# Decode attention with a 805 MB cache on one core: longer runs per transfer, all queries at the start, and another exit

## The chip, the cores and the metric

One Trainium2 chip, one of its cores. The metric is device time in microseconds (us) of one execution. A time is the median of a kernel's runs. Each ratio is the mean time of one kernel's fast runs over the mean of the other's fast runs of the same rounds, so it isn't quite the ratio of the medians quoted beside it. The profile measures a span that is 1.8 us shorter than the time of the same run.

## The reference

One token goes through a pre-norm attention block with a cache of 32,768 keys and values for each of 32 heads, then through a small MLP. All inputs are bf16.

```python
B, Sq, D = 1, 1, 640
H, Sk, Dh = 32, 32768, 192
q = (layernorm(x) @ wq).reshape(B, Sq, H, Dh).transpose(0, 2, 1, 3)
scores = einsum("bhqd,bhkd->bhqk", q, k_cache) * (Dh ** -0.5)
o = einsum("bhqk,bhkd->bhqd", softmax(scores), v_cache)
h = x + o.transpose(0, 2, 1, 3).reshape(B, Sq, H * Dh) @ wo
out = h + relu(layernorm(h) @ w1) @ w2          # w1 640 x 1536
```

K and V of all heads are 2 x 32 x 32,768 x 192 x 2 B = 805 MB. With the weights, 825 MB are read once, and nothing large is written.

## The kernel before

Each engine runs its own program. SyncE issues all loads in one order and waits where a place isn't free. GpSimd passes landings on to TensorE and VectorE. A load holds 64 keys a partition, 24 KB in one run (JL = 64). There are four key places and two value places, and a head takes four loads of each kind. A head's scores are made in eight chunks of 32 keys a partition: 16 or 20 of them on TensorE, from transposed keys that ScalarE copies out of PSUM, and the rest on VectorE. ScalarE makes the exponentials, TensorE the products with the values.

```python
kt = [sbuf(f"kt{i}", [P, JL * Dh], bf16, 512) for i in range(NL)]     # NL = 4
vt = [sbuf(f"vt{i}", [P, JL * Dh], bf16, 512) for i in range(NV)]     # NV = 2
wq_s = sbuf("wq_s", [P, DT * QG * Dh], bf16, 512)                     # wq for 8 heads
...
load(wq_v, wq_view[:, :, 0:QG * Dh], "dwq", "wq", 0)
for h in range(H):
    for ld in range(NL if h < LAST else NL - 1):
        n = NL * h + ld
        load(kt[ld][:], rows(k_hd, h, P * JL * ld, JL), f"dk{ld}", "k", h, ld)
        if n >= NV:
            hp, lp = divmod(n - NV, NL)
            g.wait("PV", hp, 2 * lp + 1)           # products out of this place are done
        load(vt[ld % NV][:], rows(v_hd, h, P * JL * ld, JL), f"dv{ld % NV}", "v", h, ld)
        # ... wq for the next 8 heads, wo for two heads
# ... the last head: the last quarter in pieces of 40, 16, 8 keys, then their values, then w1, w2
g.wait("y_row")
load(out.rearrange("b s (c p) -> (b s c) p", p=P), y_row[:], "dout", "out")
g.wait("out")
```

TensorE's order in a head puts the value products of a chunk right behind the next chunk's transposes:

```python
for c in range(NC):
    transposes(g, h, c)
    if c > 0:
        values(g, h, c - 1)
    else: ...                                       # last chunk of the head before, denominators
    scores_pe(g, h, c)
    # c == 5: q of the next head, c == 6: its broadcast
```

At the end, a context manager (`nc.cleanup_on_exit()`) clears the semaphores after a barrier behind everything else.

The softmax here doesn't subtract the row's maximum and nothing guards it: scores larger than these inputs give would overflow.

## Time and profile before

| | before |
|---|---|
| time, first three runs | 1923.66 to 1923.92 us |
| span of the profile | 1922.4 us |
| bytes read | 825 MB |
| packets on the load queue | 44,762 |
| first data packet to last w2 packet | 1912.87 us |
| last w2 packet to the output's issue | 4.12 us |
| output's issue to end of span | 3.35 us |

Rows five and six are read from the trace's DMA records: each packet has a start, a duration and a size. They split a span into loading, what comes after it, and what the engines lose between. On the page itself, a row of 9s for the DMA with lower shares for all engines says who is the bound. A queue that waits long for compute says nothing against that as long as transfers are still in flight.

### The profile page before, as it was taken

How to read it: one execution, taken by the hardware profiler on the slowest of the kernel's cores; microseconds unless marked ns; L12 is line 12 of the kernel's file. 1: busy time of each engine (PE TensorE's matmuls, PEld its weight loads, DVE VectorE, ACT ScalarE, POOL GpSimd, SP SyncE). 2: the span in 40 equal slices, each digit the busy share in tenths (PEclk: the TensorE clock that was granted, in tenths of full speed). 3: DMA queues.
4: the chain of work that ended last, by engine and by line, in shares of the span. 5: the costliest groups of instructions: out<-in, count | busy, mean ns of one | idle time of the engine just before them, and what ended most of it. 6: DMA issues, size and time to landing. Idle time of an engine off the chain costs nothing.

```text
span 1922.4 us, 36522 instructions
## 1 busy us (share of the span) xinstructions
PE 1563.5 (81%) x15899; PEld 1073.1 (56%) x15899; DVE 1560.6 (81%) x734; ACT 970.7 (50%) x2031; POOL 0.7 (0%) x6
## 2 busy tenths in 40 slices
PE   5888888788888888788787888888878887888887
PEld 4555555555555555555555555555545555555555
DVE  5878888887887888787888878888778887888886
ACT  3555455454555555454454555545445454555554
POOL 0000000000000000000000000000000000000000
PEclk9898888988888898888898888888888888898888
DMA  9999999999999999999999999999999999999998
GB/s 405 430 431 432 432 434 433 433 431 432 433 431 433 434 433 432 432 432 428 435 434 433 432 432 433 433 432 432 432 433 433 432 433 433 432 433 433 433 430 342
DMA packets 44793, 825.26 MB, mean 429 GB/s; under 512 B 4580, under 2 KB 6116, under 8 KB 12132
## 3 DMA queue, kind: packets, MB, share of 16 engines
q1 hardware_dynamic: 44762, 824.99, 99.9%
q8 instruction: 12, 0.20, 0.0%
q14 instruction: 9, 0.07, 0.0%
q10 hardware_dynamic: 10, 0.00, 0.0%
HBM read 824.97 MB, written 0.00 MB: 429 GB/s over the span
## 4 chain that ended last, share of the span: by engine, by line
DMA 76%; PE 21%; SPq 2%; issue 1%; ACT 0%; POOLq 0%; DVE 0%
DMA kt<-in_A_k_cache_dram 76%; PE o_ps L324 11%; PE tp L343 10%; SPq L224 2%; PE sp L324 0%; PE attT L324 0%; ACT kT L538 0%; POOLq L306 0%; PE mm L324 0%; DVE o_pair L638 0%; ACT pB L544 0%; PE mm L527 0%; DVE y_row L713 0%; ACT h1T L600 0%; DVE oT L648 0%
## 5 line engine op out<-in xcount | busy, mean ns | idle before, releaser
L623 DVE TENSOR_TENSOR pr<-kt,qb 128x2304 f32<-128x2304 bf16 (+2 forms) x257 | 756.0, 2942 | 278.9 <-POOLq L290 261.5
L538 ACT COPY kT<-tp 128x1024 bf16<-128x1024 bf16 (+1 forms) x899 | 818.8, 992 | 319.3 <-PE tp L343 317.3
L343 PE MATMUL tp<-ident_f,kt 128*128 128x128 f32 x3459 | 569.7, 331 | 334.3 <-POOLq L306 334.3
L626 DVE TENSOR_REDUCE sc<-pr 128x12 f32<-128x2304 f32 (+2 forms) x257 | 755.3, 2939 | 8.9
L343 PEld LDWEIGHTS tp<-ident_f,kt 128*128 128x128 f32 x3459 | 496.1, 172 | 351.3 <-POOLq L306 350.1
L324 PE MATMUL o_ps<-vt,pB 128*2 128x384 bf16 x2286 | 472.5, 358 | 6.8 <-POOLq L306 6.6
L324 PE MATMUL o_ps<-vt,pA 128*2 128x384 bf16 x1778 | 331.0, 326 | 0.0
L324 PEld LDWEIGHTS o_ps<-vt,pB 128*2 128x2 bf16 x2286 | 184.5, 89 | 244.7 <-issue 88.3
L544 ACT ACTIVATE pB<-sp 128x20 bf16<-128x20 f32 (+2 forms) x258 | 47.9, 186 | 504.5 <-PE sp L324 504.5
L324 PEld LDWEIGHTS sp<-qm,kT 128*128 128x128 bf16 x6918 | 193.3, 97 | 77.9 <-issue 65.2
L324 PEld LDWEIGHTS o_ps<-vt,pA 128*2 128x2 bf16 x1778 | 150.7, 85 | 144.9 <-issue 7.9
L324 PE MATMUL sp<-qm,kT 128*128 128x2 bf16 x6918 | 212.0, 164 | 3.1 <-ACT kT L538 2.4
L553 ACT ACTIVATE pA<-sc 128x12 bf16<-128x12 f32 (+2 forms) x257 | 53.4, 208 | 106.4 <-DVEq L65 104.7
L544 ACT ACTIVATION_READ_ACCUMULATOR pB<-sp 128x1 f32 x258 | 50.2, 195 | 0.0
L553 ACT ACTIVATION_READ_ACCUMULATOR pA<-sc 128x1 f32 x257 | 48.7, 190 | 0.0
L631 DVE TENSOR_REDUCE rec<-mm 128x1 f32<-128x20 f32 x32 | 5.7, 179 | 50.3 <-PE mm L324 49.8
L324 PE MATMUL mm<-wq_s,xn_ln 128*1 (+1 forms) x160 | 18.7, 248 | 4.0 <-POOLq L306 4.0
L638 DVE TENSOR_SCALAR o_pair<-o_ps,rec 2x384 bf16<-2x384 f32 x32 | 19.4, 605 | 2.7 <-PE o_ps L324 1.7
L324 PE MATMUL attT<-oT,wo_s 128*128 128x1 bf16 x465 | 15.9, 163 | 0.3 <-DVE oT L648 0.3
L324 PEld LDWEIGHTS mm<-dsums,ones_mat 128*128 128x128 f32 x64 | 9.5, 188 | 10.7 <-issue 9.3
L324 PEld LDWEIGHTS attT<-oT,wo_s 128*128 128x128 bf16 x465 | 13.8, 96 | 0.4 <-DVE oT L648 0.4
L324 PE MATMUL mm<-ones_row,row_e 1*128 1x1 bf16 x384 | 14.0, 159 | 0.0
(71 smaller groups left out, 144.9 us busy)
## 6 DMA issues: line engine op xcount, KB each, us to landing
kt<-in_A_k_cache_dram SPq DMA_DIRECT2D x127, 3072.0 KB, 22.5
vt<-in_A_v_cache_dram SPq DMA_DIRECT2D x127, 3072.0 KB, 15.6
wq_s<-in_A_wq_dram SPq DMA_DIRECT2D x4, 1920.0 KB, 21.0
wo_s<-in_A_wo_dram SPq DMA_DIRECT2D x16, 480.0 KB, 16.3
kt<-in_A_k_cache_dram SPq DMA_DIRECT2D x1, 1920.0 KB, 20.2
kt<-in_A_v_cache_dram SPq DMA_DIRECT2D x2, 960.0 KB, 24.8
kt<-in_B_w_dram SPq DMA_DIRECT2D x1, 1920.0 KB, 18.5
wq_s<-in_B_w_dram SPq DMA_DIRECT2D x1, 960.0 KB, 20.5
```

Of the source, the lines that this page charges most:

```text
L224: g.do(lambda: nc.sync.dma_start(out=dst, in_=src), sem, label, by=16)
L324: return lambda: pe.matmul(o, lhsT=w, rhs=r, **kw)
L343: calls.append(lambda b=b, o=o: pe.transpose(out=dst[:, b, :], in_=src[:, o:o + 2 * P].bitcast(f32), identity=ident_f[:]))
L538: g.do(lambda: act.copy(out=kT[c % 2][:, b0:b0 + nb, :], in_=src[:, 0:nb, :].bitcast(bf16)), "act_pe", ("cp", h, c, k))
L544: g.do(lambda: act.activation(out=pB[c % 4][:, 0:jp], in_=sp[:, 0:jp], func=F.Exp, scale=SCALE, accum_out=dsums[:, 2 * c + 1:2 * c + 2]), ...
L553: g.do(lambda: act.activation(out=pA[c % 4][:, 0:jd], in_=sc[c % NC][:, 0:jd], func=F.Exp, scale=SCALE, accum_out=dsums[:, 2 * c:2 * c + 1 ...
L623: g.chain(lambda: dve.tensor_tensor(out=pr[:, 0:j1 - j0, :], in0=src[:, (off + j0) * Dh:(off + j1) * Dh].rearrange("p (j d) -> p j d", d=D ...
L626: g.chain(lambda: dve.reduce_sum(out=sc[c % NC][:, j0:j1], in_=pr[:, 0:j1 - j0, :], axis=X), "dve")
L631: g.chain(lambda: dve.reduce_sum(out=rec[:, 0:1], in_=mm[:, 0:2 * NCM], axis=X), "dve")
L638: g.do(lambda: dve.tensor_scalar_mul(out=o_pair[:, :, 1, :], in0=o_ps[0:2, 0:2 * Dh].rearrange("q (i d) -> q i d", i=2), scalar1=rec[0:2, ...
```

## The change

Its intent: fewer and longer runs in each transfer, wq out of the loop so that its place can go to keys and values, and a shorter end. The key places become two of 48 KB (128 keys a partition), the values get one place of 48 KB (`va`, the second half of a head) and one of 24 KB (`vb`, used twice a head). All of wq is loaded first, into places that keys and values will take over, and all 32 queries are made at once. In the last head all keys are loaded ahead of three quarters of the values. ScalarE copies the output and sends it, and the semaphores are cleared while it flies.

```diff
-    kt = [sbuf(f"kt{i}", [P, JL * Dh], bf16, 512) for i in range(NL)]
-    vt = [sbuf(f"vt{i}", [P, JL * Dh], bf16, 512) for i in range(NV)]
-    wq_s = sbuf("wq_s", [P, DT * QG * Dh], bf16, 512)
+    kt = [sbuf(f"kt{i}", [P, JK * Dh], bf16, 512) for i in range(NK)]      # JK = 128, NK = 2
+    va = sbuf("va", [P, JK * Dh], bf16, 512)
+    vb = sbuf("vb", [P, JL * Dh], bf16, 512)
...
+    wq_c = [kt[1][:, c * H * Dh:(c + 1) * H * Dh] for c in range(DT - 1)] + [va[:, 0:H * Dh]]
...
+        def keys(h, ld):
+            if h > 0:
+                if ld == 0:
+                    g.wait("PV", h - 1, 4 if h == 1 else 2)
+                else:
+                    g.wait("PV", h - 1, 5)
+                g.wait("scs", h - 1, 4 * ld + 3)
+            elif ld == 1:
+                g.wait("att0")
+            load(kt[ld][:], rows(k_hd, h, P * JK * ld, JK), f"dk{ld}", "k", h, ld)
+
+        def vals(h, ld):
+            if ld == 1:
+                g.wait("PV", h, 1)
+            elif h > 0:
+                g.wait("PV", h - 1, 3 if ld == 0 else NC - 1)
+            src = rows(v_hd, h, P * JK * (ld // 2), JK)
+            if ld < 2:
+                src = src[:, ld * JL * Dh:(ld + 1) * JL * Dh]
+            load((vb, vb, va)[ld][:], src, "dva" if ld == 2 else "dvb", "v", h, ld)
+
+        for c in range(DT):
+            load(wq_c[c], wq_view[:, c * H * Dh:(c + 1) * H * Dh], f"dwq{c}", "wq", c)
+        for h in range(LAST):
+            keys(h, 0)
+            vals(h, 0)
+            keys(h, 1)
+            for ld in ((2, 1) if h == 0 else (1, 2)):
+                vals(h, ld)
...
+    SUMS = ((), (), (0,), (1,), (), (), (2, 3), (4,), (5, 6, 7))            # products by slot
...
+        g.wait("yT")
+        g.do(lambda: act.copy(out=y_row[:], in_=mm[0:DT, 0:P]), "act_row", ("y_row",))
+        g.wait("y_row")
+        g.do(lambda: act.dma_start(out=out.rearrange(...), in_=y_row[:]), "dout", ("out",), by=16)
...
-    ctx.enter_context(nc.cleanup_on_exit())
+    nc.clear_and_free_semaphores([n for n in nc.allocated_since(before) if n != sems["dout"].num])
+    nc.sync.wait_ge(sems["dout"], 16)
+    nc.sync.sem_inc(sems["dout"], -16)
```

Cut from the diff: the rewritten spreading of a query, TensorE's and ScalarE's orders in the last head, VectorE's signal `scs` that it has read a key place, and GpSimd's identity of another width.

## The prediction

> **What bounds the kernel now.** I read the page's utilisation rows and DMA part first, then the chain, then the issuing queue's own waits, then timelines of the two ends.
>
> ```profile
> span 1922.4 us, 36522 instructions
> PE 1563.5 (81%) x15899; PEld 1073.1 (56%) x15899; DVE 1560.6 (81%) x734; ACT 970.7 (50%) x2031; POOL 0.7 (0%) x6
> DMA  9999999999999999999999999999999999999998
> GB/s 405 430 431 432 432 434 433 433 431 432 433 431 433 434 433 432 432 432 428 435 434 433 432 432 433 433 432 432 432 433 433 432 433 433 432 433 433 433 430 342
> DMA packets 44793, 825.26 MB, mean 429 GB/s; under 512 B 4580, under 2 KB 6116, under 8 KB 12132
> q1 hardware_dynamic: 44762, 824.99, 99.9%
> DMA 76%; PE 21%; SPq 2%; issue 1%; ACT 0%; POOLq 0%; DVE 0%
> ```
>
> No compute engine is full, and the sixteen DMA engines are: every slice but the first and last moves 428 to 435 GB/s. The chain names key transfers and then two PE groups, the transposes and the value products. That PE part is not the bound: the next view shows the queue waiting for buffers, with transfers still in flight.
>
> ```profile
> SPq L224 <- PE o_ps L324: 1772.9, 126, 33.6
> ...
> kt<-in_A_k_cache_dram SPq DMA_DIRECT2D x127, 3072.0 KB, 22.5
> vt<-in_A_v_cache_dram SPq DMA_DIRECT2D x127, 3072.0 KB, 15.6
> ```
>
> A 3072 KB load takes 3.146 MB / 433 GB/s = 7.3 us alone, so 22.5 and 15.6 us from issue to landing are about three and two loads deep. The long wait of the issuing queue is back-pressure. The two ends are where the DMA does not run:
>
> ```profile
> 0.00:3.00 3.00, 0.00 (x0) 0.00 (x0) 1.32 (x8) 1.28 (x1) 0.70 (x6) 1.00 0.28 44
> ...
> 1912.00:1916.00 4.00, 3.10 (x85) 2.75 (x85) 1.56 (x11) 0.29 (x1) 0.00 (x0) 1.00 0.46 168
> 1916.00:1920.00 4.00, 2.12 (x61) 1.75 (x61) 0.44 (x2) 0.27 (x1) 0.00 (x0) 0.57 0.00 0
> 1920.00:1924.00 4.00, 0.00 (x0) 0.00 (x0) 0.00 (x0) 0.00 (x0) 0.00 (x0) 0.50 0.00 0
> ```
>
> (The last three fields are granted clock, DMA share, GB/s.) A share of 0.28 of 3 us puts the first byte at 3 - 0.84 = 2.16 us. The packet records of the trace, laid on that, end with w2 at 1915.03 us on the slowest engine (1912 + 0.46 x 4 = 1913.8 on the mean). Between, the same records leave 1.0 us of idle DMA in all. So the span is 2.2 us of start, 1912.9 of DMA, and 7.4 of end. Only three things can shorten it: less DMA time for the same bytes, less end, less start.
>
> **What a packet costs.** In the trace's packet records, the time from one packet's start to the next on the same engine is 908.4 ns for 24,576 B, 569.5 for 15,360, 146 for 3,840, 118 for 3,072, about 50 for 1,280, and 5.85 for the 4 B semaphore write. From 118 to 908.4 the slope is 790.4 ns / 21,504 B = 0.03676 ns a byte, or 27.2 GB/s an engine; what is left over is 908.4 - 24,576 x 0.03676 = about 4.9 ns a packet, whatever its size. The 24,576 B period is 908 to 909 ns from the 5th to the 95th percentile: HBM never holds it up.
>
> **What the Trainium skill says.** "DMA: Bandwidth & Descriptors", section Where 436 GB/s comes from: 16 ports x 32 B x 850 MHz = 435.2 GB/s. The trace agrees: 16 x 27.2 = 435.2, and whole slices lie just below. The same page, Why small descriptors are slow, gives a fixed overhead of some 3 cycles a packet; the trace has 4.9 ns, about 4 cycles of that clock. The section Why a DMA increments its semaphore by 16 says that one descriptor moves one contiguous run, and trouble with runs begins beyond 64 KiB; 49,152 B is below, but no packet of the kernel before is over 24,576 B on this queue, so its trace doesn't show it. Issuing engines are not separate DMA queues: a transfer issued by ScalarE runs on the same engines, so the output gains no bandwidth from that. The output is 1.2 KB; that is no matter here.
>
> **The change part by part.** Bytes stay the same (the same caches, weights and output).
>
> Packets. Before: 31 heads x 8 loads x 128 = 31,744 of 24 KB, 1,664 in the last head, wq 2,560, wo 2,048, w1 640, w2 1,536: 40,192 and some 4,565 semaphore writes, which is the page's 44,762. After: a head has K, K and the second value half as 3 x 128 packets of 48 KB and two value quarters as 2 x 128 of 24 KB: 640 instead of 1,024, over 31 heads 19,840. The last head has 1,792 (one value quarter split in two), wq 640 of 12,288 B, the rest as it was: 26,496 in all. 13,696 fewer x 4.9 ns / 16 engines = 4.2 us. Loads fall from 285 to 194: 91 x 16 semaphore writes x 5.85 ns / 16 = 0.5 us. As the DMA sets the pace, both come off in full: **-4.7 us**.
>
> The queries. Before, each head had 5 products with wq (0.57 us in the timeline), a ScalarE row copy of 0.3 and 13 small products (0.7). After, 320 products at the start and 8 small ones a head. The 60 w1 products took 1.67 us, 28 ns each, so 64 for the last wq piece are 1.8 us after its landing, and the other 256 lie under the wq loads. All of wq now stands ahead of the keys: 7.86 MB / 434 GB/s = 18.1 us, so the first keys land at some 35 us instead of 16. The PE starts later; the DMA doesn't: **0**. The relief of about 1 us a head on PE is off the path: **0**.
>
> The end. Before, all through the last 35 us PE works without a break in the chain (keys at 1883.66, last product at 1911.6), and then come the reduction, projection and MLP:
>
> ```profile
> 1911.62 0.60 DVE L638 TENSOR_SCALAR o_pair<-o_ps,rec 2x384 bf16<-2x384 f32 x1 [1.67 <-PE o_ps L324]
> ...
> 1914.34 1.65 PE L324 MATMUL o_ps<-xn_ln,kt 128*128 128x1 bf16 x60
> ...
> 1916.36 1.75 PE L324 MATMUL attT<-h1T,wq_s 128*128 128x1 bf16 x60 [0.36 <-ACT h1T L600]
> ...
> 1918.77 0.28 DVE L713 CAST y_row<-mm 5x128 bf16<-5x128 f32 x1 [0.47 <-PE mm L527]
> 1919.08 0.36 SPq L224 DMA_DIRECT2D out_dram<-y_row  x1
> ```
>
> The output is issued 4.05 us after the DMA's last byte: the tail is PE's. After, all keys of the last head are loaded before three quarters of its values, so what follows the last value bytes is only two small products. Call the DMA's end D. The last values land 3.93 MB (w1, w2) = 9.1 us before D. VectorE is the doubt: at 0.42 us a key (5.1 us for 12), its 76 to 80 keys of the last three quarters, behind a start at the first keys' landing 60 us before D, end some 10 us before D. Then 16 + 8 keys of products (1.4 + 0.8 us), so the last product is at about D - 6; 2.7 us on is w1's turn (1911.6 to 1914.34 above), D - 3.3; 2.0 us for it and the ReLU, D - 1.3; the w2 products 1.75, held at the end by w2's last landing, D + 0.7; 1.0 for y, its transpose and the copy: D + 1.7 to 2.3 with some throttling, for 4.05 now. **-2.1 us**.
>
> After the issue. Before: issue at 1919.08, end of span 1922.4, 3.3 us: 0.4 of issue, 0.8 of wait for the landing, then 0.7, 0.6 and 0.5 of barrier waits in the queue's own view, one after the other. After, barriers and clearing run while the output flies, and its semaphore alone is waited for. The longer of the two, some 2.1, remains, and ScalarE's issue is a shade slower (0.58 us for x at the start): **-0.8 us**. Copy by ScalarE (0.2 to 0.3) for VectorE (0.28): 0.
>
> **Does the queue run dry?** This is the decision. Larger places mean fewer ahead. Set one head's first key landing at 0: K takes 14.5 us, a quarter 7.2, so V0 lands at 7.2, K1 at 21.7, V1 at 28.9, V2 at 43.4, the next keys at 58. The tight wait is V1, which needs products 0 and 1 out of the same buffer. VectorE: chunk 0 to 5.2, 0.9 for the denominators, chunk 1 (6.7) to 12.8; its exponential to 13.2; products 1 to about 16. Issue and first byte take 1.2 us (0.97 to 2.16 at the start), so data can flow at 17.2, before 21.7: **4.5 us in hand**. The next K0 needs products 2, near 37, before 42: 5. K1 needs products 5, near 52, before 64: 12. But PE has four value groups after V2's landing at 43.4, with a mean of 3.16 us each (803 us / 254) plus two score groups of 0.85: to 58, just when the next keys land. So PE can be a few us late in throttled stretches, and the 4.5 us swallow it. I set **+0.5 us** for some heads that miss.
>
> **Sum.** -4.7 - 2.1 - 0.8 + 0.5 = -7.1 on 1923.79: 1916.7; I say 1916.5.
>
> **Rivals.** One: the 48 KB run is cut in two or more packets. Against it is only the 64 KiB statement. Then the 11,904 packets of the full heads come back, 3.6 us: about 1920. Two: the V1 wait bites. For it: PE's tight stretch, clock dips to 0.54 in 3 us windows. Each us missed a head is 31 us of time: at 1 us a head 1948, at 1.3 slower by 2%. Against: the 4.5 us. Three: VectorE is late in the last head, where keys come back to back, and the tail stays as it is: 1918.6. Four: a 48 KB pitch disturbs HBM; the flat 908 ns speak against it.
>
> **Range and chances.** At best, tail and barriers give 2 more: 1913.5. With rival one, or small misses, 1920 to 1922. Range 1913 to 1922. A gain of 2% is 38.5 us, more than all DMA idle and overhead together (9.6 us at the ends, 14 of packets and semaphore writes): 0.01. Slower by 2% needs 1.3 us of dry queue in each head: 0.04. Within: 0.95.
>
> **What would show it.** Packets on the queue near 26,500 + 3,100 = 29,600 (about 41,500 if cut); steady slices of 433 to 434 GB/s; DMA's end near 1910; output issued 1.7 to 2.3 us after it; span end 2.5 after issue; the first keys transposed near 35 us. Wrong if slices fall to 425 or less in mid-run, with the issuing queue's wait on the value products ending just as the engines stop.

## The result

| | before | after |
|---|---|---|
| time, six runs each | 1923.86 us (1923.65 to 1924.11) | 1918.95 us (1917.64 to 1921.12) |
| ratio | | 0.9975, 95% interval 0.9963 to 0.9988 |
| span of the profile | 1922.4 | 1916.6 |
| load packets | 44,762 | 29,600 |
| first data packet to last w2 packet | 1912.87 | 1909.47 |
| last w2 packet to the output's issue | 4.12 | 2.80 |
| output's issue to end of span | 3.35 | 2.31 |

The gain is a quarter of a per cent here, and it is outside the noise. With 15 further runs of the same kernel beside the experiments, on three chips, the median of all 21 is 1918.33 us (1916.72 to 1921.12). The kernel before had 1923.53 to 1924.89 in all its runs. What the kernel after brings besides the gain is a spread of 4.4 us.

The page of the kernel after, the same parts as those that the prediction shows:

```profile
span 1916.6 us, 36108 instructions
PE 1560.1 (81%) x15899; PEld 1093.9 (57%) x15899; DVE 1561.3 (81%) x731; ACT 938.7 (49%) x2000; POOL 1.0 (0%) x6
GB/s 409 427 435 429 429 437 429 437 434 432 436 432 435 432 433 430 434 432 437 435 430 436 433 432 434 435 429 435 431 437 435 431 435 433 432 436 432 429 432 362
DMA packets 29634, 825.29 MB, mean 431 GB/s; under 512 B 3115, under 2 KB 4652, under 8 KB 8108
q1 hardware_dynamic: 29600, 824.98, 99.8%
DVE 39%; DMA 38%; PE 16%; ACT 5%; issue 1%; DVEq 0%; POOLq 0%; SPq 0%
```

Busy times are nearly unchanged (ScalarE's falls from 970.7 to 938.7). There are a third fewer packets for the same bytes, and the mean rate rises from 429 to 431 GB/s. The chain now names VectorE first, at 39%. That doesn't make VectorE the bound: the load queue now also waits for VectorE's signal that a key place is read, so the chain goes back through it. The queue's own waits show the same thing, and its transfers are as deep in flight as before (a 6144 KB load alone takes 14.5 us):

```profile
SPq L232 <- PE o_ps L360: 1198.2, 126, 24.2
SPq L43 <- DVEq L65: 462.1, 49, 11.8
...
kt<-in_A_k_cache_dram SPq DMA_DIRECT2D x62, 6144.0 KB, 26.7
```

The end, in order of time (start, duration, engine, line, operation):

```profile
1906.85 0.60 DVE L715 TENSOR_SCALAR o_pair<-o_ps,rec 2x384 bf16<-2x384 f32 x1 [1.66 <-PE o_ps L360]
...
1911.59 1.72 PE L360 MATMUL attT<-h1T,kt 128*128 128x1 bf16 x60 [0.36 <-ACT h1T L673]
...
1913.98 0.26 ACT L676 CAST y_row<-mm 5x128 bf16<-5x128 f32 x1 [2.44 <-PE mm L592]
1914.26 0.29 ACTq L678 DMA_DIRECT2D out_dram<-y_row  x1
```

From the last product (o_pair) to the output's issue it is 7.4 us here and 7.5 before, the same work. What moved is where it stands against the last loads.

A middle head, to hold against the prediction's picture of one head. The first line is the landing of its first keys as TensorE sees it, the second the issue of its second value load, the third the landing of its second keys:

```profile
919.75 6.02 PE L379 MATMUL tp<-ident_f,kt 128*128 128x128 f32 x27 [2.71 <-POOLq L342]
...
936.02 0.33 SPq L232 DMA_DIRECT2D vb<-in_A_v_cache_dram  x1
...
941.55 3.46 PE L379 MATMUL tp<-ident_f,kt 128*128 128x128 f32 x15 [3.60 <-POOLq L342]
```

Issued 16.3 us after the first keys (predicted 17.2 less 1.2 of issue, so 16), with the other keys landing at 21.8 (predicted 21.7). The 2.71 in the bracket is TensorE's idle time ahead of the keys: it wasn't late there.

### The profile page after: what moved, and what is told of

Same layout as the page of the kernel before. It is cut to its first block, busy times and chain, and to the rows that moved or that the text cites. A ratio compares the mean times of both kernels' runs of the same rounds, so it can differ in the third digit from the quotient of the medians.

```text
span 1916.6 us, 36108 instructions
## 1 busy us (share of the span) xinstructions
PE 1560.1 (81%) x15899; PEld 1093.9 (57%) x15899; DVE 1561.3 (81%) x731; ACT 938.7 (49%) x2000; POOL 1.0 (0%) x6
## 3 DMA queue, kind: packets, MB, share of 16 engines
q1 hardware_dynamic: 29600, 824.98, 99.8%
## 4 chain that ended last, share of the span: by engine, by line
DVE 39%; DMA 38%; PE 16%; ACT 5%; issue 1%; DVEq 0%; POOLq 0%; SPq 0%
DMA kt<-in_A_k_cache_dram 35%; DVE sc L703 19%; DVE pr L700 18%; PE o_ps L360 8%; PE tp L379 7%; ACT kT L603 5%; DMA va<-in_A_v_cache_dram 2%; PE sp L360 1%; DVE o_pair L715 1%; ACT pA L618 1%; DVE oT L725 0%; DMA kt<-in_A_wq_dram 0%; DVE rec L708 0%; DVE rec L709 0%; DVE odd L721 0%
## 5 line engine op out<-in xcount | busy, mean ns | idle before, releaser
L379 PE MATMUL tp<-ident_f,kt 128*128 128x128 f32 x3456 | 595.7, 334 | 241.3 <-POOLq L342 166.5
L360 PE MATMUL o_ps<-va,pB 128*2 128x384 bf16 x1152 | 219.9, 339 | 55.5 <-POOLq L342 55.5
L360 PE MATMUL o_ps<-vb,pB 128*2 128x384 bf16 x1152 | 217.1, 335 | 23.1 <-ACT pA L618 22.5
L360 PEld LDWEIGHTS o_ps<-va,pB 128*2 128x2 bf16 x1152 | 94.0, 86 | 150.4 <-POOLq L342 62.9
L360 PE MATMUL o_ps<-va,pA 128*2 128x384 bf16 x896 | 172.9, 335 | 0.0
L360 PE MATMUL o_ps<-vb,pA 128*2 128x384 bf16 x896 | 166.7, 326 | 0.0
L360 PEld LDWEIGHTS o_ps<-vb,pB 128*2 128x2 bf16 x1152 | 91.0, 85 | 125.6 <-ACT pA L618 28.3
L360 PEld LDWEIGHTS o_ps<-va,pA 128*2 128x2 bf16 x896 | 77.4, 86 | 75.9 <-issue 9.4
L360 PEld LDWEIGHTS o_ps<-vb,pA 128*2 128x2 bf16 x896 | 75.4, 84 | 70.2
L360 PE MATMUL o_ps<-xn_ln,kt 128*96 128x1 bf16 (+1 forms) x316 | 22.3, 208 | 2.8 <-DMA kt<-in_A_wq_dram 2.8
## 6 DMA issues: line engine op xcount, KB each, us to landing
kt<-in_A_k_cache_dram SPq DMA_DIRECT2D x3, 3072.0 KB, 22.7
```

The lines of the kernel that those rows point to most:

```text
L360: return lambda: pe.matmul(o, lhsT=w, rhs=r, **kw)
L379: calls.append(lambda b=b, o=o: pe.transpose(out=dst[:, b, :], in_=src[:, o:o + 2 * P].bitcast(f32), identity=ident_f[:]))
```

## The experiments

Twelve runs, three of them of the kernel after itself. All passed the comparison with the reference, also the one that leaves out products: what it drops is too little of the sum to show.

### The time per packet

Twice, once in each kernel. In the kernel after, each 48 KB run is loaded as two of 24 KB by two transfers into the same place, on the same waits:

```diff
-            load(kt[ld][:], rows(k_hd, h, P * JK * ld, JK), f"dk{ld}", "k", h, ld)
+            src = rows(k_hd, h, P * JK * ld, JK)
+            for i in range(2):
+                s = slice(i * JL * Dh, (i + 1) * JL * Dh)
+                load(kt[ld][:, s], src[:, s], f"dk{ld}", "k", h, ld)      # and so for va
```

> Theory one, the time per packet: every 48 KB run is loaded as two runs of 24 KB by two transfers, into the same places, on the same waits. 93 places x 128 = 11,904 more packets x 4.9 ns / 16 = 3.6 us, and 93 x 16 more semaphore writes x 5.85 ns / 16 = 0.5 us: 4.2 us slower than the changed kernel (3.5 to 5), packets on the queue near 43,000. Rival: the gain came from the waits and the ends, and packet sizes are hidden: within 1 us of the changed kernel.

In the kernel before, each 24 KB run becomes two of 12 KB:

```diff
-                load(kt[ld][:], rows(k_hd, h, P * JL * ld, JL), f"dk{ld}", "k", h, ld)
+                w = JL * Dh // 2
+                for i in range(2):
+                    load(kt[ld][:, i * w:(i + 1) * w], rows(k_hd, h, P * JL * ld, JL)[:, i * w:(i + 1) * w], ...)
```

> The kernel before with each 24 KB run loaded as two of 12 KB (but for the last pieces of the last head): about 254 x 128 = 32,000 more packets x 4.9 ns / 16 = 9.9 us and 254 x 16 semaphore writes x 5.85 ns / 16 = 1.5 us, so 11.4 us slower: 1935. Rival that packets cost nothing while the memory sets the rate: within 1 us.

The load queue's line of the page, first of the kernel after with runs cut, then of the kernel before with runs cut:

```profile
q1 hardware_dynamic: 42992, 824.99, 99.9%
```

```profile
q1 hardware_dynamic: 81338, 825.00, 100.3%
```

The kernel before became 1935.68 us against 1924.32 in the same rounds: 11.4 us slower, where 11.4 was expected (ratio 1.006, interval 1.0047 to 1.0074). The kernel after became 1921.56 against 1917.06, 4.5 us slower for an expected 4.2. That pair is the weaker one: two of the five runs with runs cut took 1924.65 and 1924.82, so the means differ by 5.2. The packet records are steadier. From the first data packet to the last w2 packet it is 1914.28 us there, beside 1909.41 to 1910.14 in four profiles of the kernel after (4.1 to 4.9 more), and 1924.46 against 1912.87 in the kernel before (11.6 more). Nothing but the number of packets and of transfers was changed in either, so their time is real, adds up, and isn't hidden. The runs double both together; how the cost splits between packets and semaphore writes is read from the records alone. For the 49,152 B packets of the kernel after, the trace has 1812 ns from start to start, twice 908 less 4, as the model of 4.9 ns a packet has it (1807.1 + 4.9). The rival that the run would be cut in two is out: 11,904 packets of 49,152 B are in the trace.

### The exit

The kernel after with the old exit (VectorE copies, SyncE sends and waits, barrier and clearing last):

```diff
-        g.do(lambda: act.copy(out=y_row[:], in_=mm[0:DT, 0:P]), "act_row", ("y_row",))
-        g.do(lambda: act.dma_start(out=..., in_=y_row[:]), "dout", ("out",), by=16)
+        g.do(lambda: dve.tensor_copy(out=y_row[:], in_=mm[0:DT, 0:P]), "act_row", ("y_row",))
+        load(out.rearrange(...), y_row[:], "dout", "out")       # SyncE; then g.wait("out")
+    ctx.enter_context(nc.cleanup_on_exit())                     # in place of the new clearing
```

> The changed kernel with the old exit: VectorE copies the output row, SyncE sends it, waits for it and only then come the barriers and the clearing. Theory: from the output's issue to the end of the span 3.3 us again instead of 2.34: 0.9 to 1.0 us slower than the changed kernel. Rival: the end of the program waits for something else, no difference.

And the kernel before with the new exit alone (the same edit the other way round):

> The kernel before with the new exit alone (ScalarE copies and sends the output, semaphores but one are cleared while it flies). The kernel before has a spread of half a us, so this measures the exit alone: 0.8 to 1.0 us faster, 1922.9. Rival: no difference.

With the old exit the kernel after took 1918.41 us against 1917.06, 1.35 more; but the medians of the kernel after itself differ by 1.9 from set to set, so this pair alone shows little. The kernel before with the new exit took 1922.59 against 1924.32, 1.7 less; its ratio, 0.9992 with an interval of 0.9978 to 1.0006, doesn't exclude zero, so the trace has to carry it. There, all that isn't between the first data packet and the output's issue falls from 5.43 to 4.36 us, 1.07 less, and rises from 4.30 to 5.42 where the old exit was put back. So the exit is worth 1.1 us, and the rest of the 1.7 is not explained.

### How much is in hand at the tight wait

The prediction's rival two said that the second value load waits for product 1, and that each us too late would cost 31 us. Here it is made too late: it also waits for VectorE's fourth chunk.

```diff
             if ld == 1:
                 g.wait("PV", h, 1)
+                g.wait("scs", h, 3)
```

> The wait that the prediction called tight, made tighter: the second value load of each head also waits for VectorE's fourth chunk, which in a middle head ends at 26.1 us after the first keys land, where the product that it waits for now lets the issue go at 16.4. The queue's work ends at 21.7. Theory: issue and first byte take 1.2 us, so the engines are dry for 26.1 + 1.2 - 21.7 = 5.6 us a head, in 31 heads some 170 us; less if the compute engines catch up in the gap (VectorE starts a head only when the keys land, so it does not): 1060 to 1100 above 1000, that is 2050 to 2100 us. Rival: the queue has more in hand than the landings show and hides it, under 1950.

It took 2142.69 us (ratio to the kernel before 1.1138): 224 us above the kernel after, 7.2 for each of 31 heads, where 5.6 was expected. The same three events of a middle head, first keys, second keys, second value load:

```profile
1023.71 2.41 PE L380 MATMUL tp<-ident_f,kt 128*128 128x128 f32 x19 [0.77 <-POOLq L343]
...
1045.48 3.46 PE L380 MATMUL tp<-ident_f,kt 128*128 128x128 f32 x15 [3.58 <-POOLq L343]
1049.82 0.33 SPq L232 DMA_DIRECT2D vb<-in_A_v_cache_dram  x1
```

And four us of it by engine (PE, PEld, DVE, ACT, POOL, then granted clock, DMA share, GB/s):

```profile
1044.00:1048.00 4.00, 2.52 (x12) 2.52 (x13) 3.97 (x2) 0.00 (x0) 0.00 (x0) 0.50 0.00 0
```

The issue is at 26.1 us after the first keys, as expected. What I had left out: the engines' last packets of the second keys end between 1043.91 and 1045.11, 0.4 to 1.6 us before TensorE sees the landing at 1045.48, and 1.1 in the mean. And 30 heads ran dry, not 31: in the first head the 48 KB of values are loaded ahead of the second value quarter. So the engines stood idle 6.7 us in each of the 30 (203.1 us in all), not 5.6. And when sixteen idle engines start together, their first packets take longer than usual: the excess over the usual durations sums to 24.3 us, of which 0.76 behind each dry stretch, where the kernel after has 2.2 in all. 30 x (6.7 + 0.76) = 224 us, what was lost. The mechanism of the rival is shown, and what the change has in hand is some 3.2 us, not 4.5: 21.8 less 16.3, less 1.2 to the first byte, less about 1.1 for the landing.

### Head 1, where the queue nearly ran dry

Counting the bytes issued and not yet moved at each issue, the kernel after has one weak place, the first keys of head 1, which wait for the first half-speed products of head 0:

```profile
74.05 3.36 PE L360 MATMUL o_ps<-va,pB 128*2 128x384 bf16 x10 [4.92 <-POOLq L342]
...
79.36 0.33 SPq L232 DMA_DIRECT2D kt<-in_A_k_cache_dram  x1
```

Less than 1 us of transfers was left there. The place is in truth free when TensorE's fourth transposes are done, one product group earlier:

```diff
-                    g.wait("PV", h - 1, 4 if h == 1 else 2)
+                    g.wait("PV", h - 1, 1)
```

> The first key place of the next head is asked for one value group earlier (product 1 instead of 2, in head 1 instead of 4), which is when its last transpose is done; nothing else changes. The trace showed the queue down to some 0.8 us of work when the keys of head 1 were issued, and stretched packets after it. Theory: 0.5 to 1 us faster than the changed kernel, DMA end near 1910.8 in place of 1911.6, and if head 1 is what spreads the runs, a spread under 1 us. Rival: the queue never ran dry there, no difference in median or spread.

The stretched packets between 78 and 84 us (0.63 us in the kernel after) fell to 0, and from the first to the last packet it took 1908.67 us instead of 1909.47. But the time was 1919.11 us (1916.82 to 1919.19) beside 1917.06 for the kernel after on the same chip: no gain in the runs, and no smaller spread. The near-dry place is real, about half a us of packet time, and it isn't what spreads the runs.

### What sets the tail

Half of the products of chunks 2 to 5 of the last head are left out, so the result is wrong:

```diff
+        if h == LAST and 2 <= c <= 5:
+            order = order[::2]
```

> Wrong result on purpose: in the last head half of the value products of chunks 2 to 5 are left out, 5.4 us of TensorE after the second value load lands. Theory: TensorE sets the changed kernel's tail (2.63 us from the DMA's last byte to the output's issue, where the DMA alone would allow some 1.3), so the issue comes about 1.2 us earlier against the DMA's end: 1.3 to 1.5 us after it. Rival: the weights' landing already sets it, no difference.

The output was issued 1.71 us after the last w2 packet, against 2.80, 2.44, 1.89 and 4.22 in four profiles of the kernel after; 1.3 to 1.5 was expected. (The 2.63 of the expectation is the 2.80 of the table.) One profile, 0.2 us under the lowest of four, would be thin evidence; what carries the reading is the chain. The piece of the chain before the last w2 products is now the w2 load:

```profile
1895.08 15.61 DMA kt<-in_B_w_dram
1910.69 0.05 issue
1910.74 0.44 PE attT L360 x10
```

In the four profiles of the kernel after, the last load in the chain ends between 1865 and 1888, and from there on the chain is compute. So compute sets its tail, which falls short of what the loads allow. The runs moved little: 1917.09 us against 1918.3, with a spread of 2 us.

### A better order, and the clock

In the kernel after, ScalarE's copies of transposes fill 1872 to 1888 without a break, TensorE waits on them, and the clock falls to half just before the products come. Columns as above:

```profile
1880.00:1884.00 4.00, 3.23 (x45) 2.97 (x45) 3.82 (x3) 4.00 (x11) 0.00 (x0) 0.68 1.03 444
1884.00:1888.00 4.00, 3.91 (x45) 3.04 (x43) 3.96 (x2) 4.00 (x12) 0.00 (x0) 0.50 0.88 378
1888.00:1892.00 4.00, 4.00 (x15) 1.64 (x14) 3.85 (x2) 0.96 (x2) 0.00 (x0) 0.54 1.01 426
```

The Trainium skill, "TensorE: Matmul & The Clock Gate", part 1, section What's actually happening, says that a monitor passes half or all of the clock by how busy TensorE has been in a free-running window of 3413 ns. The trace agrees: its clock records have only 0.5 and 1.0, in multiples of 3413 ns. Two kernels act on it. The first loads the second value quarter of the last head ahead of the last two key quarters and does products 2 to 5 between the transposes (with the earlier key wait of the run above):

```diff
-        transposes(g, h, 4)
-        scores_pe(g, h, 3)
+        values(g, h, 2)
+        transposes(g, h, 4)
+        scores_pe(g, h, 3)          # and so on: 3 behind the transposes of 6, 4 of 8, 5 of 9; 9 ahead of 8
```

> An attempt at a better version: the changed kernel with the earlier key issue of the run before, and in the last head the second value load put ahead of the last two key quarters, so that products 2 to 5 are done while ScalarE copies transposes, and the smallest product, which needs no VectorE scores, ahead of the last. Theory that TensorE's products after the last keys set the tail: output issued 1.3 to 2.0 us after the DMA's last byte instead of 2.0 to 2.8, about 1 us faster than the changed kernel (1916 to 1917.5 where that takes 1917 to 1919), and a smaller spread. Rival: VectorE's last scores, now started later, hold the last product and the tail stays as it was.

> The changed kernel once more, beside the attempt, on its chip. Expected: 1917 to 1919 us; runs with a higher mean granted clock are the faster ones, as in the first ten (0.885: 1916.7 to 1917.6; 0.876 to 0.880: 1918.4 to 1921.1)[...].

The other fills TensorE's gaps in the kernel after with products that nobody reads, into unused columns of a PSUM bank that only TensorE uses then:

```diff
+    def warm(g):                    # called after the transposes of chunks 3 to 9
+        for _ in range(5):
+            g.do(mmul(attT[:, 128:416], ident_b, wide[:, 0:288], start=True, stop=True, skip_group_check=True))
```

> The changed kernel with idle work: in the last head, five products of 288 columns that nobody reads after each of the transposes of chunks 3 to 9, about 0.6 us of TensorE each time at full clock, in the stretch where TensorE waits for ScalarE's copies. The trace's clock records come in windows of 3.41 us, and in five profiles of this tail the last dip to half speed before the end lasted one to four of them; the longer, the later the output (1910.8, 1911.3, 1911.9, 1912.3 and 1912.3 us after the first byte for 3.4, 6.8, 10.2, 10.2 and 13.7 us). Theory: gaps on TensorE bring the dip, so with them filled no dip or one window falls between 1880 and 1896, the output is issued at 1910.5 to 1911 after the first byte, and the runs lie within 1 us of each other, near 1917. Rival: the dips come on their own, or the extra 4 us of TensorE work costs more than the dip: no gain or a loss, spread as before.

> The changed kernel beside the filled one, on its chip: 1917 to 1919 us, a spread of 1.5 to 3 us, and in its profile a dip of one to four windows of 3.41 us shortly before 1895.

And the kernel after for the first time, beside the packet runs:

> The changed kernel as it is, as an anchor for the kernels beside it and for its own spread. Expected: 1919 us median, runs between 1917.5 and 1921, ratio 0.997 to 0.998 to the kernel before. If the spread of 3.5 us comes from the clock's dips in a tail that TensorE sets, the profile taken here shows the output issued at another distance from the DMA's end than 2.63 us; if it comes from a queue that runs dry in head 1, the DMA's end itself moves and its idle time is found near 80 us.

The profiles of this tail but for that of the late wait, in us. "Half speed" is the sum of the clock records at 0.5 between 1860 and 1895; the last column is the median of the kernel's runs and their range.

| kernel | first data packet to last w2 packet | from there to output's issue | half speed | time |
|---|---|---|---|---|
| after, first set | 1909.47 | 2.80 | 10.2 | 1918.95 (1917.64 to 1921.12) |
| after, beside packets | 1909.86 | 2.44 | 13.7 | 1917.06 (1916.72 to 1918.71) |
| after, beside better order | 1909.41 | 1.89 | 6.8 | 1917.76 (1917.37 to 1918.55) |
| after, beside filled | 1910.14 | 4.22 | 10.2 | 1918.33 (1917.47 to 1920.45) |
| old exit | 1908.78 | 1.97 | 3.4 | 1918.41 (1917.93 to 1918.86) |
| earlier key wait | 1908.67 | 3.26 | 10.2 | 1919.11 (1916.82 to 1919.19) |
| 48 KB runs cut | 1914.28 | 4.21 | 14.6 | 1921.56 (1921.42 to 1924.82) |
| half of the products 2 to 5 | 1908.43 | 1.71 | 13.7 | 1917.09 (1916.22 to 1918.25) |
| better order | 1908.63 | 2.29 | 6.8 | 1917.24 (1916.63 to 1917.50) |
| filled gaps | 1910.20 | 1.79 | 3.4 | 1917.69 (1916.36 to 1919.83) |

Filling did what it should to the clock in this stretch:

```profile
1880.00:1884.00 4.00, 3.87 (x77) 3.48 (x75) 3.82 (x3) 4.00 (x7) 0.00 (x0) 1.00 1.02 433
1884.00:1888.00 4.00, 3.67 (x58) 2.90 (x57) 3.96 (x2) 4.00 (x13) 0.00 (x0) 1.00 0.93 396
1888.00:1892.00 4.00, 4.00 (x29) 2.25 (x29) 3.85 (x2) 2.48 (x8) 0.00 (x0) 1.00 1.01 425
```

The first product group there (chunk 2) takes 2.7 us instead of 4.6. In the chain, first of the kernel after, then of the filled one:

```profile
1887.85 4.60 PE o_ps L360 x16
```

```profile
1889.33 2.69 PE o_ps L360 x16
```

All eight profiles of the unfilled tail have a dip between 1877 and 1898 us, the filled one has none there. It has TensorE busy for 92% or more of each window of 3413 ns from 1868 to 1906; in the kernel after it is 73% in the window ahead of the dip. But two windows of 73 and 70% shortly before (from 1857.6 us) brought no dip, so the records give no threshold. And the expected 1 us of spread didn't come (3.5 us), nor the expected issue at 1910.5 to 1911 after the first packet (1911.99). In the filled profile a window of half speed still lay at 1865 to 1868, before the filling begins, on the transposes that start ScalarE's copies (3.34 us there, 1.86 in the kernel after), and the last five idle products stand in the chain with 0.61 us of their own. So gaps on TensorE bring the dips as far as one filled profile can show it, dips do lengthen the tail, and they aren't the whole spread. In the profile of 1920.45 us, one window of half speed lay at 1866, on the transposes that start ScalarE's copies, and two at 1886 to 1893; its copies ended 2.5 us later than in the first profile, 0.9 of it because the keys landed later (first transposes at 1866.09, not 1865.17) and 1.6 because these transposes took 3.43 us, not 1.86. Where in the last head a window falls seems to count as much as how many there are. The mean clock and the time of the 21 runs of the kernel after go together (correlation -0.67), which fits and proves nothing more. What else spreads the DMA's part by 1.6 us between profiles stays open.

The better order has the smallest spread (0.9 us in five runs, though the old exit's five had 0.9 too) and a ratio of 0.9963 to the kernel before, beside 0.9967 for the kernel after in the same rounds, with intervals that overlap almost wholly. It isn't shown to be faster.

## Why the prediction was right

The time lies in its range (1913 to 1922), 2.4 us above the number said. That alone says little, for the range is wider than the gain, and rival three's number, 1918.6, is nearer to the median than 1916.5. What supports the mechanism is its terms and the experiments. By its own terms, on the two profiled runs (whose difference is 5.8 us; the medians differ by 4.9):

| term | predicted | measured |
|---|---|---|
| packets and semaphore writes | -4.7 | -4.74 by the records' counts; experiments 11.4 for 11.4, 4.5 for 4.2 |
| heads that run dry | +0.5 | none dry in mid-run; other DMA losses +1.3 |
| tail after the last byte | -2.1 | -1.3 (over four profiles -2.2 to +0.1) |
| after the output's issue | -0.8 | -1.0 |
| start | 0 | -0.1 |
| sum | -7.1 | -5.8 in span |

No run undoes the order of the last loads or the early queries alone; what the table has for the tail and the start is read off the traces.

**Packets.** The data packets are 26,496, as counted in advance, and the semaphore writes 3,104. The step rested on one number that the trace had and the page hasn't, the time from packet to packet by size, and it held in three kernels. The skill's overhead of about 3 cycles a packet came out as 4.9 ns.

**What the DMA lost.** First to last packet fell by 3.4, not by 4.2. Idle time rose by about 0.3 us, packets that took longer than usual from 1.30 to 2.24 us in all (0.67 in the first 20 us, 0.63 where head 1 nearly ran dry), and the rest lies in engines that end at different times. The term was there, under "some heads that miss", but with another cause and at under half of what was lost (0.5 for 1.3).

**The tail.** This step failed in part. It had VectorE as the doubt, only 16 + 8 keys of products left behind its last scores, the last product at D - 6 (D is the DMA's end), and the w2 products "held at the end by w2's last landing, D + 0.7". The trace has another path: ScalarE's copies are the bound until 1886 us, then products 2 to 9 follow each other almost without a break from 1887.85 to 1906.83, which is D - 4.6. The w2 products end at D + 1.9 and no landing holds them. The first of the product groups ran at half clock and took 4.6 us instead of 2.7. So the tail is 2.80 us, and 1.89 to 4.22 over four profiles, for 1.7 to 2.3. With half of the products of four chunks out it was 1.71 with w2's landing in the chain, as the step has it.

**The tight wait.** The product came at 16.3 us as worked out and the queue kept its hold. The reserve was overstated by about 1.1 us, because the engines are done before the landing is seen. That didn't matter to this kernel and would to one with less in hand.

**The queries.** 28 ns a product was wrong: the last 164 of them took 13.1 us, 80 ns each (19.85 to 32.97 in the timeline). The second keys were issued at 33.2, with the queue full to about 42, so it was off the path as the step said.

**Signs and sums.** Of its signs, the packets came exactly (29,600), the output 2.8 us after the DMA's end for 1.7 to 2.3, the end of the span 2.3 after the issue for 2.5, and the first keys were transposed at 37.69 us for 35. Two of its figures are off, and nothing rests on them: packets of 1,280 B follow each other at 52 ns, not about 50, and from 1916.5 it takes 1.5 us a head to be slower by 2%, not 1.3.

**The rivals.** Cut runs: no; that 48 KB stay whole is shown by the trace, the sentence on 64 KiB is about longer rows only. The tight wait: shown to cost 7.5 us in each of the 30 heads where it was made to bite, and in the kernel after it didn't bite. VectorE late in the last head: not in the chain. A 48 KB pitch that disturbs HBM: no, the packets of 48 KB follow each other at 1811 ns at the 5th percentile and 1813 at the 95th.

## What to carry to other kernels

When loads bound a kernel and HBM keeps up, read the packet records. A fixed time per packet times the number of packets over 16 engines is a gain that could here be computed to half a us in advance, and it was the largest of the terms. Before making places larger and fewer, find the one wait with the least in hand and count from the last packet's end on the engines, not from the landing that compute sees; a queue that runs dry costs its idle time and some more for the restart. The end of this kernel is bound by compute, and behind a thin stretch of TensorE it ran at half clock just when it counted, in all eight profiles of this order.

## What the Trainium skill lacked or had wrong

- "DMA: Bandwidth & Descriptors", section Why small descriptors are slow: the fixed cost is put at 3 cycles and as a matter of small descriptors. Measured: 4.9 ns (4 cycles of 850 MHz) for every packet from 3,072 to 49,152 B, worth 4.2 us in this kernel at 24 to 48 KB, and 5.85 ns for each semaphore write.
- The same page, section Where 436 GB/s comes from, says that for loads the HBM side (about 358 GB/s a core) binds. For a core alone that doesn't hold, as the 425 GB/s that the page itself measured with one core says: here a core alone ran at 432 to 437 GB/s in most slices, at the port limit of 435.2 within what a slice resolves.
- No page has the restart of a dry queue: 0.76 us of stretched packets each time on top of the idle time (30 restarts, 22.7 us). Nor has one a number for the time from the engines' last packets to TensorE acting on the landing, for loads that SyncE issues: 0.4 to 1.6 us here, 1.1 in the mean.
- "TensorE: Matmul & The Clock Gate", part 1, section What's actually happening, has the window of 3413 ns and the half clock; both agree with the records. Its table puts the half clock behind at least one idle window. Here TensorE was 73% busy in the window ahead of the dip at 1881.4 us, with no gap over 0.8 us, and the records have some 470 us of 1917 at half clock in a kernel whose TensorE is 81% busy. (Further down the page tells of dips from short idle times too, without a number for them.) Products that nobody reads, put into the gaps, kept the clock full from 1868 to 1909 us.
